# Gate and up projections: two blocks of 64 channels stacked on the 128 rows of TensorE, in place of gate on one half of the rows and up on the other

## The chip, the cores and the metric

The kernel runs on one core of a Trainium2 chip. Its instructions stand in five queues, each run in order: TensorE (PE in the profile, with its weight loads shown apart as PEld), VectorE (DVE), ScalarE (ACT), GpSimd (POOL) and SyncE (SP), which here issues all DMAs. The metric is the device time of one execution in microseconds (us), and the lower the better. It is given as the median of several runs. One further execution is profiled; all durations below come from it.

## The reference, cut to what matters

```python
x = x + ga * _A_ref(h, ...)      # spectral block over 8192 tokens of 448 channels, h = layernorm(x)*(1+ca)+sa
h = _layernorm(x, axis=-1) * (1 + cb) + sb
x = x + gb * ((_gelu(h @ w_gate) * (h @ w_up)) @ w_down)   # w_gate, w_up 448 x 1792; w_down 1792 x 448
```

The change concerns `h @ w_gate` and `h @ w_up` of the last line, what prepares their operands, and the traffic between memory and SBUF that goes with them. The spectral block, GELU and `w_down` are computed as before.

## The kernel before, in words

The first part (up to about 450 us in the profile) computes the spectral block in units of its own and, beside it, prepares the weights. The second part (450 us to the end) is the feed-forward loop.

**The loop.** The 8192 tokens make 32 chunks of two token groups of 128. The 1792 hidden features make seven tile pairs t of two times 128. A unit u is one chunk with one tile pair, so there are 224 units, and `period(u)` writes out the work around each. Odd chunks take the tile pairs in reverse (`torder`), so that some weights are still in SBUF.

**Seven products for eight.** For a unit, gate and up are each a product of 2 token groups x 448 channels with 448 channels x 2 tiles. The 448 channels are seven blocks of 64: two halves of three blocks (192 channels) and a rest of one. The halves are multiplied by Winograd's form of Strassen's scheme: seven products of halves in place of eight, with sums of weights (`form_sums`: S1 to S4) and of tokens (`token_sums`: t1 to t4). Each operand is split in f16 into a high and a low part, and each product adds three terms: high by high, weight high by token low, weight low by token high. `RV`, `RY`, `RX` are three regions of a PSUM set into which the products are added.

**Half rows.** Gate's weights lie in SBUF on partitions 0 to 63 and up's on 64 to 127. `mm` (L1171 to L1184, the product at L1177) issues, for each block of 64 channels and each of the three terms, one product on the upper 64 rows of the array (gate) and one on the lower 64 (up), each of 64 rows x 128 weights with 128 tokens. A unit has 25 blocks (`stage_a` 9, `stage_d` 4, `stage_c` 9, `stage_b` 3), so 25 x 3 x 2 = 150 products, each with a weight load of its own. As the block is needed on both halves of the rows, the tokens are transposed twice, shifted by 64 columns (`nt`, 2 x 24 blocks of 128 x 128, by DMA transposes at L1161).

**The order.** Within period u each engine takes: `stage_a(u)`, then on the unit two back `joins` (DVE, L1223 and L1229: PSUM plus a copy), `gel3` (ACT, L1235), `mult3` (DVE, L1239), `stage_d(u-2)`, `gel1` (ACT, L1243), `mult1` (DVE, L1246) and `sums` (POOL, L1250 to L1253), further `quant_hi(u-3)` (ACT, L1258) and `quant_lo(u-4)` (DVE, L1267), then `stage_c(u-1)` and `stage_b(u)`. `stage_d(u-2)` writes where `joins(u-2)` reads, so TensorE waits for it. `seed` and `copy_b` are ACT's copies L1218 and L1214. With k = u mod 7, the lists `extra` and `first` add the preparation of later chunks: `split_v`, `split_g` (k = 1), `transposes` of the next chunk (k = 1 to 4), `token_sums` (k = 3, 4) and packing into f16 (`pack_hi` on ACT, `pack_lo` on POOL, k = 3 to 6). After period k = 2, `phase` issues the `inverse` of the chunk after next (L1066 to L1068, 6 products) and `down` of the chunk before: 147 products with 224 columns each (L1277 to L1279), full rows.

**Weights.** The seven tile pairs do not all fit, so four slots hold them; after the last use in a chunk, `after` and `flush` put a reload on SP's queue (L1032, three parts). They come from a DRAM copy that the first part wrote (`store_forms`, L830). Tile pairs 0 and 1 are formed last and stay in the two slots in which they were formed.

Of the kernel before, what the change touches and what calls it, by code (L numbers as in the profile page):

```python
# [34 lines left out]
WPARTS = (12, 6, 5)  # L35
NWB = sum(WPARTS)
NXB = 48
NXT = NXB // 2
# [8 lines left out]
def spectral_geglu(ctx, tc, x, w1, b1, w2, b2, wg, wu, wd, cvec, wmod, cf1, cs2, cmi, cgm, out):  # L47
# [11 lines left out]
    wsd = [dram.tile([NP, 128, 2, n, 128], F16, name=f"wsd{n}") for n in WPARTS]  # L59
# [261 lines left out]
    with ExitStack() as bctx:  # L321
# [472 lines left out]
        def load_forms(t):  # L794
            r = fp.tile([128, 14, 128], F32, tag="wr", name="wr", bufs=2)
            for pr, rows in enumerate(rows2):
                v = (wg, wu)[pr].rearrange("(k p) (q t f) -> p q k t f", p=64, q=2, t=NP)
                for q in range(2):
                    dma(r[rows, 6 * q : 6 * q + 6], v[:, q, 0:6, t])
                dma(r[rows, 12:14], v[:, :, 6, t])  # L800
            return r

        def form_sums(t):
            r = raws[("w", t)]
            f = raws[("f", t)] = fp.tile([128, 9, 128], F32, tag="wf", name="wf")
            a11, a12, a21, a22 = (r[:, 3 * j : 3 * j + 3] for j in range(4))
            G.tensor_tensor(f[:, 3:6], a11, a21, ALU.subtract)
            G.tensor_tensor(a21, a21, a22, ALU.add)
            G.tensor_tensor(f[:, 0:3], a21, a11, ALU.subtract)
            G.tensor_tensor(f[:, 6:9], a12, f[:, 0:3], ALU.subtract)  # L810

        def form_cuts(t, part):
            r = raws[("w", t)]
            if part == 0:
                return (slice(0, 9), r[:, 0:9]), (slice(18, 23), r[:, 9:14])
            return ((slice(9, 18), raws[("f", t)]),)

        def forms_hi(t, part):
            for k, src in form_cuts(t, part):
                S.activation(wslot[wat[t]][:, 0, k], src, AF.Copy, scale=sww)  # L820

        def forms_lo(t, part):
            for k, src in form_cuts(t, part):
                w = wslot[wat[t]]
                V.scalar_tensor_tensor(w[:, 1, k], src, sww, w[:, 0, k], op0=ALU.mult, op1=ALU.subtract)

        def store_forms(t):
            a = 0
            for w, n in zip(wsd, WPARTS):
                dma(w[t], wslot[wat[t]][:, :, a : a + n])  # L830
                a += n
# [52 lines left out]
        wpool = ctx.enter_context(tc.tile_pool(name="wpool", bufs=1))  # L884
        wslot = [wpool.tile([128, 2, NWB, 128], F16, name=f"ws{s}") for s in range(2)]
# [85 lines left out]
        fp = fctx.enter_context(tc.tile_pool(name="fp", bufs=1))  # L971

# [28 lines left out]
    with ExitStack() as cctx:  # L1001
        cp = cctx.enter_context(tc.tile_pool(name="cp", bufs=1, side="right"))
        wslot += [cp.tile([128, 2, NWB, 128], F16, name=f"ws{s}") for s in (2, 3)]
# [5 lines left out]
        pkt = cp.tile([128, (NXB + 1) * 64], F16, name="pk")  # L1009
# [5 lines left out]
        def plan_slots():  # L1015

            held = [[0 if wat[0] == s else 1, -1] for s in range(2)] + [[2, -1], [3, -1]]
            for u, t in enumerate(torder):
                s = next((n for n, (h, _) in enumerate(held) if h == t), None)
                if s is None:  # L1020
                    s = min(range(4), key=lambda n: held[n][1])
                    refill[held[s][1]] = u
                    held[s][0] = t
                slot_of[u] = wslot[s]
                held[s][1] = u
# [3 lines left out]
        def load_part(u, part):  # L1029

            lo, n = sum(WPARTS[:part]), WPARTS[part]
            dma(slot_of[u][:, :, lo : lo + n], wsd[part][torder[u]])  # L1032
# [84 lines left out]
        def token_sums(i, part):  # L1117

            n = nxt[i]["n"]
            if part == 0:  # L1120
                nxt[i]["t"] = cp.tile([128, 13 * 64], F32, tag="tf", name="tf")
# [3 lines left out]
            t1, t2, t3, t4 = (t[:, 192 * j : 192 * j + 192] for j in range(4))  # L1125
            if part == 0:
                V.tensor_tensor(t1, b12, b11, ALU.subtract)  # L1127
                V.tensor_tensor(t3, b22, b12, ALU.subtract)
            else:
                V.tensor_tensor(t2, b22, t1, ALU.subtract)  # L1130
                V.tensor_tensor(t4, b21, t2, ALU.subtract)
                V.tensor_tensor(t[:, 768:832], x0, x1, ALU.subtract)

        def pieces(i, k):
            n, h = nxt[i]["n"], 448
            if k == 0:
                return n[:, 0], 0, 448, 448
            if k == 1:
                return n[:, 1, 192:448], 896, 256, 256
            t, a, b = nxt[i]["t"], *((0, 416), (416, 832))[k - 2]  # L1140
            return t[:, a:b], 1408 + a, 832, b - a

        def pack_hi(i, ks):
            for k in ks:
                src, o, _, w = pieces(i, k)
                S.copy(pkt[:, o : o + w], src)
                if k == 0:
                    S.copy(pkt[:, NXB * 64 :], src[:, 0:64])

        def pack_lo(i, ks, e=G):  # L1150
            for k in ks:
                src, o, d, w = pieces(i, k)
                e.tensor_tensor(pkt[:, o + d : o + d + w], src, pkt[:, o : o + w], ALU.subtract)

        def transposes(i, gs, w=4):
            if i not in nts:
                nts[i] = cp.tile([128, 2, NXT, 128], F16, tag="nt", name="nt", bufs=2)
            for g in gs:
                sw_, c = divmod(g, NXT // w)
                o, n = 64 * sw_ + 128 * w * c, 128 * w  # L1160
                nc.sync.dma_start(nts[i][:, sw_, w * c : w * c + w, :], pkt[:, o : o + n], transpose=True)  # L1161

        XB0, XB1, XT = (0, 7), (14 - 3, 18 - 3), (22, 35)

        def xblock(i, pr, n):
            w, odd = divmod(n, 2)
            if odd == pr:
                return nts[i][rows2[pr], 0, w, :]
            return nts[i][rows2[pr], 1, w if odd else (w - 1) % NXT, :]

        def mm(u, ps2, reg, wb, x, xo, n, start=False):  # L1171

            i, slot = u // NP, slot_of[u]
            for j in range(n):
                for m, (hl, xb) in enumerate(((0, x[0]), (0, x[1]), (1, x[0]))):
                    for pr, rows in enumerate(rows2):
                        T.matmul(  # L1177
                            ps2[:, pr, reg * 128 : reg * 128 + 128],
                            slot[rows, hl, wb + j, :],
                            xblock(i, pr, xb + xo + j),  # L1180
                            start=start and j == 0 and m == 0,
                            stop=j == n - 1 and m == 2,
                            skip_group_check=True,
                        )  # L1184

        RV, RY, RX = 0, 1, 2

        def stage_a(u):
            p = sets[u % 3]
            mm(u, p, RY, 0, XB0, 0, 3, start=True)  # L1190
            mm(u, p, RV, 6, XT, 0, 3)
            mm(u, p, RX, 3, XB0, 3, 3)

        def stage_b(u):
            mm(u, sets[u % 3], RY, 9, XT, 3, 3)

        def stage_c(u):
            p = sets[u % 3]
            mm(u, p, RV, 12, XT, 6, 3)
            mm(u, p, RV, 22, XB1, 6, 1)  # L1200
            mm(u, p, RY, 15, XB1, 3, 3)
            mm(u, p, RY, 21, XB1, 6, 1)
            mm(u, p, RX, 21, XB0, 6, 1)

        def stage_d(u):
            p = sets[u % 3]
            mm(u, p, RV, 18, XT, 9, 3)
            mm(u, p, RV, 22, XT, 12, 1)
# [127 lines left out]
        def period(u):  # L1336
# [8 lines left out]
            on(u - 2, lambda v: after(v, 2))  # L1345
# [5 lines left out]
            on(u - 1, lambda v: after(v, 1))  # L1351
# [7 lines left out]
        def phase(i):  # L1359
# [33 lines left out]
            2: [(token_sums, 1, 1), (pack_hi, 1, [2, 3]), (pack_lo, 1, [2, 3]), (transposes, 1, [0, 2], 12)],  # L1393
            3: [(transposes, 1, [1, 3], 12), ("inverse", 2), (residual, 2)],
# [3 lines left out]
            7: [(token_sums, 2, 1), (pack_hi, 2, [2, 3]), (pack_lo, 2, [2, 3])],  # L1398
        }
# [15 lines left out]
        cp2 = cctx.enter_context(tc.tile_pool(name="cp2", bufs=1))  # L1415
        loads(1)
        for part in range(len(WPARTS)):
            load_part(2, part)
        for b in range(CB):
            norm2(0, b)  # L1420
            if b == 0:
                pack_hi(0, [0])
                pack_lo(0, [0])
        token_sums(0, 0)
        token_sums(0, 1)
        pack_hi(0, [2, 3])
        pack_hi(0, [1])
        pack_lo(0, [2, 3], V)
        pack_lo(0, [1])
        S.copy(gb_r, gb[:, :D])  # L1430
        transposes(0, range(4), 12)
        for part in range(len(WPARTS)):
            load_part(3, part)
# [103 lines left out]
```

## Time and profile before

| | before |
|---|---|
| median of 3 runs | 2095.89 us (2095.4 to 2103.03) |
| the profiled execution, its own time | 2103.25 us |
| its span, first to last instruction | 2101.4 us |
| first product of the loop (L1177) | 449.65 us |
| mean granted TensorE clock | 0.969 of full speed |
| VectorE, ScalarE, GpSimd busy | 70%, 49%, 53% of the span |
| DMA: packets, bytes, share of the 16 engines | 390171, 358.5 MB, about 73% |

Times in rows of the trace are in us from the start of the span. A row of the timeline has start, length, engine, line, operation, output<-inputs, shape, count, and in brackets the idle time of the engine before it and what ended it. "issue" means that the engine waited for nothing that the profile shows. A matmul's record runs some 200 ns longer than the time until the next one can start, as they are pipelined. So the pace of a row with n matmuls is its length, less one record, by n - 1.

### The profile page before, as it was taken

What the parts mean: (1) busy time and instruction counts of PE and PEld (TensorE: products, weight loads), DVE (VectorE), ACT (ScalarE), POOL (GpSimd) and SP (SyncE); (2) the same over time, 40 slices, a digit from 0 to 9 for tenths busy, and PEclk for the clock granted to TensorE, in tenths of its full rate; (3) what the DMA queues carried; (4) which work ended last, traced back from release to release, by engine and by line L of the source; (5) the groups of instructions that cost most, each with busy time, mean ns of one, the idle gap of its engine ahead of it and who ended that gap; (6) DMA issues with size and microseconds to landing.
All of it is one profiled execution on the core that took longest, in us unless ns stands there. A gap on an engine that the chain in (4) does not pass through costs nothing.

```text
span 2101.4 us, 93045 instructions
## 1 busy us (share of the span) xinstructions
PE 1871.1 (89%) x41348; PEld 1781.5 (85%) x41348; DVE 1479.4 (70%) x2958; ACT 1029.4 (49%) x1917; POOL 1116.5 (53%) x1529
## 2 busy tenths in 40 slices
PE   7899878768989999899899998999989999999998
PEld 3699877757989888888898998898889889888998
DVE  8577777757767767666677776777667667677645
ACT  5587776634444444444444444444444444444433
POOL 3166666425555556555555655555555556555533
PEclk9899988979999999999999999999999999999999
DMA  9998688687766667767666677877666667777671
GB/s 344 305 283 244 163 237 235 184 233 177 148 148 148 148 148 148 148 148 148 148 148 148 161 158 149 154 158 156 148 148 148 148 148 164 150 166 147 142 157 40
DMA packets 390171, 358.48 MB, mean 171 GB/s; under 512 B 223876, under 2 KB 341256, under 8 KB 389768
## 3 DMA queue, kind: packets, MB, share of 16 engines
q1 hardware_dynamic: 389768, 352.53, 71.3%
q8 instruction: 323, 5.29, 1.1%
q14 instruction: 80, 0.66, 0.2%
HBM read 244.24 MB, written 57.80 MB: 144 GB/s over the span
## 4 chain that ended last, share of the span: by engine, by line
PE 69%; DVE 17%; issue 6%; DMA 3%; ACT 2%; SPq 2%; POOL 0%; ACTq 0%; DVEq 0%; POOLq 0%
PE set L1177 35%; PE pdn L1277 4%; PE pdn L1279 4%; PE pdn L1278 4%; PE set L1279 3%; PE set L1277 3%; PE set L1278 3%; DVE x L1239 3%; DVE c L1223 2%; DVE ac L1267 2%; PE ps L204 2%; DVE y L465 1%; DVE c L1229 1%; DVE tf L1127 1%; DMA g<-cgm 1%
## 5 line engine op out<-in xcount | busy, mean ns | idle before, releaser
L1177 PE MATMUL set<-nt,ws 64*128 64x128 f16 x33600 | 996.5, 218 | 147.9 <-issue 100.7
L1177 PEld LDWEIGHTS <-ws 64*128 64x128 f16 x33600 | 968.0, 95 | 176.9 <-issue 167.0
L1267 DVE SCALAR_TENSOR_TENSOR ac<-x,sa_act,ac 128x896 f16<-128x896 f32 x224 | 318.6, 1422 | 16.0 <-ACT ac L1258 15.9
L1235 ACT ACTIVATE gl<-c,dg 128x384 f32<-128x384 f32 x224 | 137.7, 615 | 370.8 <-DVE c L1229 358.3
L1223 DVE TENSOR_TENSOR c<-set,sb 128x512 f32<-128x512 f32 x224 | 153.6, 686 | 120.4 <-PE set L1177 111.6
L1277 PE MATMUL pdn<-wd,ac 128*128 128x224 f16 x896 | 233.6, 261 | 1.1 <-issue 0.6
L1279 PE MATMUL pdn<-wd,ac 128*128 128x224 f16 x896 | 233.1, 260 | 1.2 <-DVE ac L1267 1.2
L1278 PE MATMUL pdn<-wd,ac 128*128 128x224 f16 x896 | 233.1, 260 | 0.0
L1258 ACT ACTIVATE ac<-x,sa_act 128x896 f16<-128x896 f32 x224 | 231.4, 1033 | 0.5 <-DVE x L1253 0.4
L1250 POOL TENSOR_TENSOR x<-x 128x128 f32<-128x128 f32 x223 | 106.0, 475 | 221.6 <-DVE x L1239 221.6
L1239 DVE TENSOR_TENSOR x<-c,gl 128x384 f32<-128x384 f32 x224 | 198.9, 888 | 28.2 <-ACT gl L1235 28.0
L1321 POOL TENSOR_TENSOR o<-u,p 128x224 f32<-128x224 f32 x32 | 21.1, 659 | 325.9 <-DVE u L1320 325.9
L1214 ACT COPY sb<-set 128x512 f32<-128x512 f32 x224 | 129.8, 580 | 102.7 <-PE set L1177 102.4
L1277 PE MATMUL set<-wd,ac 128*128 128x224 f16 x672 | 174.0, 259 | 0.1
L1279 PE MATMUL set<-wd,ac 128*128 128x224 f16 x672 | 174.0, 259 | 0.0
L1278 PE MATMUL set<-wd,ac 128*128 128x224 f16 x672 | 174.0, 259 | 0.0
L1277 PEld LDWEIGHTS <-ac 128*128 128x128 f16 x1568 | 153.9, 98 | 8.2 <-issue 6.7
L1279 PEld LDWEIGHTS <-ac 128*128 128x128 f16 x1568 | 153.8, 98 | 2.0 <-DVE ac L1267 1.7
L1278 PEld LDWEIGHTS <-ac 128*128 128x128 f16 x1568 | 154.0, 98 | 1.3 <-issue 1.0
L465 DVE SCALAR_TENSOR_TENSOR y<-pm,t 64x224 f32<-64x224 f32 x256 | 99.5, 389 | 59.6 <-ACT t L457 55.9
L1246 DVE TENSOR_TENSOR x<-set,gl 128x128 f32<-128x128 f32 x224 | 63.9, 285 | 94.5 <-ACT gl L1243 94.1
L109 POOL TENSOR_TENSOR yl<-y,yh 128x448 fp32r<-128x448 f32 x63 | 81.1, 1287 | 92.3 <-ACT yh L107 74.1
(293 smaller groups left out, 3684.8 us busy)
## 6 DMA issues: line engine op xcount, KB each, us to landing
ws<-wsd SPq DMA_DIRECT2D x98, 768.0 KB, 5.5
ws<-wsd SPq DMA_DIRECT2D x98, 384.0 KB, 5.6
ws<-wsd SPq DMA_DIRECT2D x98, 320.0 KB
tr<-td SPq DMA_DIRECT2D x64, 224.0 KB, 5.5
vd<-us SPq DMA_DIRECT2D x64, 224.0 KB, 3.0
xx<-in_A_x SPq DMA_DIRECT2D x32, 448.0 KB, 6.0
v<-vd SPq DMA_DIRECT2D x63, 224.0 KB, 3.6
out<-x SPq DMA_DIRECT2D x31, 448.0 KB, 2.7
```

The lines of the kernel that those rows point to most:

```text
L465: V.scalar_tensor_tensor(y[ri * 64 : ri * 64 + 64, gi], pv[si, ri], LAM, tv[si, ri], op0=ALU.add, op1=ALU.min)
L1177: T.matmul(ps2[:, pr, reg * 128 : reg * 128 + 128], slot[rows, hl, wb + j, :], xblock(i, pr, xb + xo + j), start=start and j == 0 and m == ...
L1214: S.copy(sbs[u], sets[u % 3][:, :, 0:256])
L1223: V.tensor_tensor(c[:, :, 1:3, :], p[:, :, 0:256].rearrange("p g (r c) -> p g r c", r=2), b[:, :, 0:128].rearrange("p g (o c) -> p g o c", ...
L1235: S.activation(gls[u], cts[u][:, 0], AF.Gelu_apprx_tanh, scale=dg)
L1239: V.tensor_tensor(xs[u][:, 1::3, :], cts.pop(u)[:, 1], gls.pop(u), ALU.mult)
L1250: e.tensor_tensor(s1, a21, a22, ALU.add)
L1258: S.activation(acts[u][:, 0], xs[u][:, 0:7], AF.Copy, scale=sa_act[:, t : t + 1])
L1267: V.scalar_tensor_tensor(acts[u][:, 1], xs.pop(u)[:, 0:7], sa_act[:, t : t + 1], acts[u][:, 0], op0=ALU.mult, op1=ALU.subtract)
L1277: T.matmul(ps, ac[:, 0, ka], w[:, 0, kb], start=n == 0, stop=False)
L1278: T.matmul(ps, ac[:, 0, ka], w[:, 1, kb], start=False, stop=False)
L1279: T.matmul(ps, ac[:, 1, ka], w[:, 0, kb], start=False, stop=n == NP - 1)
```

## The change

Each product now uses all 128 rows: two blocks of 64 channels of the same projection stand one above the other. Gate and up become two products in turn (`pr`) with weights of their own. A product of halves has three blocks and three terms, 9 half tiles, and takes 5 full-row products (A11, S1, S2); with the rest block it has 12 half tiles and takes 6 (A12, S4, S3, A22). That is (3 x 5 + 4 x 6) x 2 = 78 products per unit, of 128 rows x 128 weights with 128 tokens. In the 5-product form the third block's token tile holds its high part above its low part.

What goes with it:

- The tokens need one layout of 25 blocks, transposed once, by 5 DMA transposes of 5 blocks per chunk and no longer 12 of 4. All are issued at k = 1 and 2. `pieces` packs five pieces, some with two strided parts; GpSimd makes 7 subtractions per chunk where there were 4, and one copy of 64 columns more.
- A tile pair's weights in SBUF are 2 x 2 x 14 tiles (projection, high or low part, form), 14336 bytes per partition, where there were 11776. They are reloaded in two parts of 1024 descriptors each (1024 and 768 bytes), where there were three of 256 (3072, 1536, 1280 bytes).
- `store_forms` writes a tile pair by 16 DMAs and no longer 3, `load_forms` reads the raw weights by 10 and no longer 6. The forms are made in two staging buffers of their own, so tile pairs 0 and 1 are loaded from DRAM at the start of the loop as well.

```diff
-WPARTS = (12, 6, 5)
-NWB = sum(WPARTS)
-NXB = 48
-NXT = NXB // 2
+NWB = 23
+WPARTS = ((0, 4), (4, 7))
+NXT = 25
...
         def store_forms(t):
-            a = 0
-            for w, n in zip(wsd, WPARTS):
-                dma(w[t], wslot[wat[t]][:, :, a : a + n])
-                a += n
+            w = wstage[wat[t]]
+            for pr, rows in enumerate(rows2):
+                top, low = (wk[t, r, pr] for r in rows2)
+                dma(top[:, :, 0:7], w[rows, :, 0:7])
+                dma(top[:, :, 7:14], w[rows, :, 14:21])
+                dma(low[:, :, 0:7], w[rows, :, 7:14])
+                dma(low[:, :, 8:11], w[rows, :, 15:18])
+                for f, b in ((7, 21), (11, 21), (12, 22), (13, 22)):
+                    dma(low[:, :, f], w[rows, :, b])
...
-            lo, n = sum(WPARTS[:part]), WPARTS[part]
-            dma(slot_of[u][:, :, lo : lo + n], wsd[part][torder[u]])
+            view = lambda w: w.rearrange("p r l (g f) x -> p (r l g) f x", g=2)[:, :, slice(*WPARTS[part])]
+            dma(view(wslot[slot_of[u]]), view(wk[torder[u]]))
...
-        def mm(u, ps2, reg, wb, x, xo, n, start=False):
-
-            i, slot = u // NP, slot_of[u]
-            for j in range(n):
-                for m, (hl, xb) in enumerate(((0, x[0]), (0, x[1]), (1, x[0]))):
-                    for pr, rows in enumerate(rows2):
-                        T.matmul(
-                            ps2[:, pr, reg * 128 : reg * 128 + 128],
-                            slot[rows, hl, wb + j, :],
-                            xblock(i, pr, xb + xo + j),
...
+        def mm(u, reg, f, x, start=False):
+
+            ps2, slot, nt = sets[u % 3], wslot[slot_of[u]], nts[u // NP]
+            if f in (A11, S1, S2):
+                terms = [(0, f, x), (0, f, x + 2), (1, f, x), (0, 7 + f, x + 1), (1, 7 + f, x + 1)]
+            else:
+                terms = [(l, f + 7 * g, x + g + 2 * m) for g in range(2) for l, m in ((0, 0), (0, 1), (1, 0))]
+            for j, (hl, wt, xt) in enumerate(terms):
+                for pr in range(2):
+                    T.matmul(
+                        ps2[:, pr, reg * 128 : reg * 128 + 128],
+                        slot[:, pr, hl, wt, :],
+                        nt[:, xt, :],
...
         def stage_a(u):
-            p = sets[u % 3]
-            mm(u, p, RY, 0, XB0, 0, 3, start=True)
-            mm(u, p, RV, 6, XT, 0, 3)
-            mm(u, p, RX, 3, XB0, 3, 3)
+            mm(u, RY, A11, B11, start=True)
+            mm(u, RV, S1, T1)
+            mm(u, RX, A12, B21)
...
-            1: [(2, split_v), (2, split_g), (1, transposes, [0, 6])],
-            2: [(1, transposes, [1, 7, 11, 5, 2, 8])],
-            3: [(1, transposes, [3, 9]), (2, token_sums, 0), (2, pack_hi, [0]), (2, pack_lo, [0])],
-            4: [(1, transposes, [4, 10]), (2, token_sums, 1), (2, pack_hi, [1]), (2, pack_lo, [1])],
-            5: [(2, pack_hi, [2]), (2, pack_lo, [2])],
-            6: [(2, pack_hi, [3]), (2, pack_lo, [3]), (3, load_v)],
+            1: [(2, split_v), (2, split_g), (1, transposes, [0])],
+            2: [(1, transposes, range(1, 5))],
+            3: [(2, token_sums, 0), (2, pack_hi, [0, 1]), (2, pack_lo, [0, 1])],
+            4: [(2, token_sums, 1), (2, pack_hi, [2]), (2, pack_lo, [2])],
+            5: [(2, pack_hi, [3]), (2, pack_lo, [3])],
+            6: [(2, pack_hi, [4]), (2, pack_lo, [4]), (3, load_v)],
```

With the other stages likewise: `stage_b` is S2, `stage_c` S3 and S4, `stage_d` A22. So in products the stages have 32 (a), 12 (d), 24 (c) and 10 (b), where they had 54, 24, 54 and 18.

**SP's queue at the start of the loop.** Before, from the store of the tile pair formed last (wsd_60 to wsd_62 are its three parts in DRAM) to the first transposes:

```order
L830 DMA wsd_60<-ws_3352 256x1x1536
L830 DMA wsd_61<-ws_3352 256x1x768
L830 DMA wsd_62<-ws_3352 256x1x640
L934 DMA v<-vd 128x2x224 x2
L926 DMA g<-cgm 128x256
L928 DMA xx<-in_A_x 128x896
L1032 DMA ws_5801<-wsd_60 128x2x1536
L1032 DMA ws_5801<-wsd_61 128x2x768
L1032 DMA ws_5801<-wsd_62 128x2x640
L1161 DMA_TRANSPOSE nt<-pk 128x12x128 x4
```

Now (the second half of the tile pair's store, then as far; the first half has the same five rows; wk_5916 and wk_5917 are the slots of units 0 and 1):

```order
L836 DMA wk<-ws_3365 64x2x896
L837 DMA wk<-ws_3365 64x2x896
L838 DMA wk<-ws_3365 64x2x896
L839 DMA wk<-ws_3365 64x2x384
L841 DMA wk<-ws_3365 64x2x128 x4
L942 DMA v<-vd 128x2x224 x2
L934 DMA g<-cgm 128x256
L936 DMA xx<-in_A_x 128x896
L1041 DMA wk_5916<-wk 128x8x512
L1041 DMA wk_5916<-wk 128x8x384
L1041 DMA wk_5917<-wk 128x8x512
L1041 DMA wk_5917<-wk 128x8x384
```

The five transposes follow it. So thirteen more stores and one more load stand ahead of the first transposes, and the weights of units 0 and 1 are loaded where they lay in SBUF.

**SP's queue in one chunk of the loop.** Before, around the output of one chunk (`out<-x`, issued at the end of `down`):

```order
L1032 DMA ws_5801<-wsd_60 128x2x1536
L1161 DMA_TRANSPOSE nt<-pk 128x4x128 x6
L1328 DMA out<-x_5897 128x896
L1032 DMA ws_3352<-wsd_62 128x2x640
L1032 DMA ws_5801<-wsd_61 128x2x768
L1161 DMA_TRANSPOSE nt<-pk 128x4x128 x2
L1032 DMA ws_5801<-wsd_62 128x2x640
L1161 DMA_TRANSPOSE nt<-pk 128x4x128 x2
```

Now, at the same place:

```order
L1175 DMA_TRANSPOSE nt<-pk 128x5x128
L1041 DMA wk_5984<-wk 128x8x384
L1041 DMA wk_5916<-wk 128x8x512
L1175 DMA_TRANSPOSE nt<-pk 128x5x128 x4
L1334 DMA out<-x_8019 128x896
L1041 DMA wk_5917<-wk 128x8x384
L1041 DMA wk_5916<-wk 128x8x384
```

The transposes that stood behind the output of the chunk before (k = 3 and 4) now stand ahead of it, and each tile pair has two reloads and no longer three.

More of the change, by code (lines that the diff above doesn't have):

```diff
@@ L58, in spectral_geglu @@
     sd = dram.tile([NP, 128, 4, HC], F32, name="sd")
[L59 removed]
+    wk = dram.tile([NP, 128, 2, 2, 14, 128], F16, name="wk")
     cpool = ctx.enter_context(tc.tile_pool(name="cpool", bufs=1))
@@ L971, in spectral_geglu @@
         fp = fctx.enter_context(tc.tile_pool(name="fp", bufs=1))
+        wstage = [fp.tile([128, 2, NWB, 128], F16, name=f"ws{s}") for s in range(2)]
         at(18, "dve", down_scales)
```

149 lines of the change are left out of this document (75 added, 74 removed).

## The prediction

> **What bounds the kernel now.** I read the page first: how busy TensorE is, whose work makes up the chain that ended last, and how many instructions there are.
>
> ```profile
> span 2101.4 us, 93045 instructions
> PE 1871.1 (89%) x41348; PEld 1781.5 (85%) x41348; DVE 1479.4 (70%) x2958; ACT 1029.4 (49%) x1917; POOL 1116.5 (53%) x1529
> q8 instruction: 323, 5.29, 1.1%
> PE 69%; DVE 17%; issue 6%; DMA 3%; ACT 2%; SPq 2%; POOL 0%; ACTq 0%; DVEq 0%; POOLq 0%
> L1177 PE MATMUL set<-nt,ws 64*128 64x128 f16 x33600 | 996.5, 218 | 147.9 <-issue 100.7
> ```
>
> TensorE carries the chain, over a third of it with the products that are changed. But 6% of the chain is "issue", and the products' largest idle time has that name. The second view is TensorE's timeline over one chunk, with the first product after a `down` early and late in the loop:
>
> ```profile
> 530.51 0.68 PE L1177 MATMUL set<-nt,ws 64*128 64x128 f16 x18 [0.48 <-DVE o L1325]
> ...
> 1151.75 10.06 PE L1177 MATMUL set<-nt,ws 64*128 64x128 f16 x354 [0.48 <-DVE o L1325]
> 1162.55 4.82 PE L1177 MATMUL set<-nt,ws 64*128 64x128 f16 x158 [0.73 <-DVE c L1229]
> 1167.92 11.07 PE L1177 MATMUL set<-nt,ws 64*128 64x128 f16 x384 [0.54 <-issue]
> 1179.15 3.97 PE L1177 MATMUL set<-nt,ws 64*128 64x128 f16 x128 [0.17 <-issue]
> 1184.27 0.90 PE L1177 MATMUL set<-nt,ws 64*128 64x128 f16 x26 [1.15 <-issue]
> 1185.10 0.47 PE L1066 MATMUL set<-vh,gh 128*128 128x448 f32 x1
> ...
> 2010.40 0.79 PE L1177 MATMUL set<-nt,ws 64*128 64x128 f16 x22 [0.48 <-DVE o L1325]
> ```
>
> From 530.51 to 2010.40 lie 29 chunks (periods 10 to 213), 51.03 us each. I cut a chunk in three: **A**, from the first product to `stage_d` in the period k = 5 (here 1151.75 to 1162.55, 10.80 us); **B**, the rest of the products; **C**, inverse, `down` and the wait for DVE, until the next first product (1201.18). The windows view gives the engines in A, B, C of that chunk:
>
> ```profile
> 1151.75:1162.55 10.80, 10.06 (x354) 9.92 (x354) 10.08 (x17) 6.41 (x14) 9.97 (x14) 1.00 0.68 124
> 1162.55:1185.10 22.55, 20.59 (x697) 19.64 (x696) 16.59 (x24) 15.40 (x28) 13.99 (x22) 1.00 0.64 174
> 1185.10:1201.18 16.08, 15.60 (x156) 15.15 (x154) 9.19 (x30) 0.97 (x3) 4.82 (x7) 1.00 0.78 155
> ```
>
> Columns: window, length, then busy time (and count) of PE, PEld, DVE, ACT, POOL; last the clock and DMA. **A** is VectorE's: 10.08 of 10.80 busy (`token_sums`), and TensorE waits at its end (0.73 us for DVE c). **B** is TensorE's, as DVE needs 16.6, ACT 15.4, POOL 14.0 of 22.55 us. **C** is `down`.
>
> What is "issue"? Two rows of another chunk:
>
> ```profile
> 1026.62 3.75 PE L1177 MATMUL set<-nt,ws 64*128 64x128 f16 x128 [1.65 <-issue]
> 1033.67 0.21 PE L1177 MATMUL set<-nt,ws 64*128 64x128 f16 x1 [3.29 <-issue]
> ...
> q8 instruction: 272, 4.46, 1.3%
> ```
>
> Between two such waits stand 128 products, and 384 = 3 x 128 in the chunk above. The DMA queue q8 brings instructions (its rows give packets, MB and share): 5.29 MB over the 2 x 41348 of TensorE is 64 bytes each, and 5.29 MB over 323 packets is 16 KB, or 256 instructions: 128 products with their weight loads. So TensorE runs a block empty, and the next is not there. From 530.51 to 2010.40 (last row) that is 272 blocks, 9.4 per chunk. Products run at (3.75 - 0.21)/127 = 27.9 ns, so a block lasts 3.57 us, and 3.57 + 3.29 = 6.9 us is the slowest refill of these rows.
>
> The Trainium skill ("Runtime: NRT & Kernel Launch", Instruction fetch mechanics) has the same 16 KiB blocks of 256 instructions, but calls their cost mostly hidden. By that rule these waits would be something else, and the change would not touch them; the trace's runs of 128 speak against it. It is the slower rival below.
>
> **The change part by part.**
>
> *Pace of a product.* A pair of half-row products runs at the same time: 2 x 27.9 = 55.8 ns. What does one full-row product with 128 columns cost? The first part has some, 24 in a row from L370 to L372, and full 128 x 128 loads at L716:
>
> ```profile
> 269.62 0.22 PE L370 MATMUL ps<-s,th 128*112 128x128 f16 x1
> ...
> 270.90 0.22 PE L372 MATMUL ps<-s,tl 128*112 128x128 f16 x1
> ...
> 200.77 0.48 PE L716 MATMUL pw<-onesb,sq 128*128 128x1 bf16 x7
> ...
> L716 PE MATMUL pw<-onesb,sq x112: 163/164/179, 118.1 to 219.3; 128*128 128x1 bf16 x84, 64*128 64x1 bf16 x28
> ...
> L1277 PEld LDWEIGHTS <-ac 128*128 128x128 f16 x1568 | 153.9, 98 | 8.2 <-issue 6.7
> ```
>
> 23 steps in 1.28 us: 55.7 ns, each with its own full-row load. The L716 products have one column and a record of 163 ns (second L716 row, minimum); seven in 0.48 us come every (0.48 - 0.16)/6 = 53 ns, so a 128-wide load needs no more than that. So 55.7 ns, hence 78 x 55.7 = 4.34 us per unit for 75 x 55.8 = 4.18: **the products by themselves get 4% longer**. Bounds: 55.7, and 98 ns (the record of a 128 x 128 load in `down`, last row) if loads were not hidden.
>
> *Part A.* TensorE needs 2 x 78 + 32 = 188 products, 10.47 us, under 10.80; DVE's instructions there are the same, so A stays 10.80. POOL's packing there changes a little: three subtractions of 64, 128 and 256 columns where one of 448 stood, and a copy of 64 columns more.
>
> ```profile
> L1250 POOL TENSOR_TENSOR x<-x 128x128 f32<-128x128 f32 x223 | 106.0, 475 | 221.6 <-DVE x L1239 221.6
> ```
>
> At 0.48 us for 128 columns that is some 0.5 us more on 9.97 of 10.80 busy. DVE's order does not wait for it, but POOL beside DVE may lengthen DVE's instructions: 0 to 0.5, I take 0.
>
> *Part B.* 46 products are left of the period k = 5, then 4 x 78: 358 x 55.7 = 19.95 us. Before, 348 pairs made 19.4. The remaining ~3.1 us of 22.55 in this chunk were waits; in the mean chunk B is 51.03 - 10.80 - 16.08 = 24.15 (fetches in A and C counted in it), so 4.7 are.
>
> *Do the waits go?* A block now holds 128 full-row products, 128 x 55.7 = 7.13 us, and the slowest refill above took 6.9. Per chunk 699 products make 5.5 blocks. I expect nearly all to go and leave 0.2 us per chunk. Bounds: none go (4.7 left), or all.
>
> *Part C.* Same instructions, 16.08; TensorE's change of tile shape (64 rows to 128) falls away: the last half product starts 0.21 before the end of its row, at 1184.96, and the inverse 0.14 later, where a step is 0.06. That is 0.1 us.
>
> Chunk after: 10.80 + 20.15 + 16.0 = 46.95, **4.08 less, times 29 = 118 us**. The last chunk (from 2010.40) runs into the end of the program, and I take half of a chunk's gain for it: 2 us.
>
> *What then stands late.* In B, DVE has 16.6 us of work for 20.0, ACT 15.4, POOL 14.0 plus some packing: all fit, DVE the tightest.
>
> *DMA.* Transposes fall from 48 to 25 blocks per chunk, weights rise by 14336/11776 = 1.22 in bytes and in packets of 1 KB for 3 KB. Both lie behind three or more periods (13 us) between slot free and next use:
>
> ```profile
> ws<-wsd SPq DMA_DIRECT2D x98, 768.0 KB, 5.5
> nt<-pk SPq DMA_TRANSPOSE x368, 5.1
> ```
>
> Landing after 5.5 us leaves over 7 us. If reloads took three times as long, `stage_a` would wait; 0 to 3 us per chunk, and I take 0.
>
> *The start.* These rows set when the loop begins:
>
> ```profile
> 432.18 3.60 SPq L830 DMA_DIRECT2D wsd<-ws  x3
> 435.88 1.81 SPq L934 DMA_DIRECT2D v<-vd  x2
> 438.79 2.03 SPq L1032 DMA_DIRECT2D ws<-wsd  x3
> 442.55 9.67 SPq L1161 DMA_TRANSPOSE nt<-pk  x4
> 454.59 1.68 PE L1177 MATMUL set<-nt,ws 64*128 64x128 f16 x28 [4.68 <-DMA nt<-pk]
> ```
>
> Sixteen stores at about 0.6 us (a `v` load takes 0.9, a part load 0.7) are 9.6 for 3.6; four loads for three, 0.7 more. The transposes start 6 to 7 us later, but 5 of 5 blocks are shorter than 4 of 12, and the first stage needs three of them: 2 to 5 us late, I take 3. In the first part each tile pair puts 17 more DMAs on SP, some 10 us at 0.6 each, and SP has idle time there:
>
> ```profile
> SPq L516 <- ACT us L499: 68.6, 13, 8.8
> ```
>
> (waits of SP from 200 to 450 us): 0 to 15 us in all, I take 3. The added fixed costs of strided forms on ACT and DVE are under 1 us. The first ten periods, 449.65 to 530.51, also lose fetch waits, but are DVE's in large part; I take 0.
>
> **Sum.** 2103.25 - 118 - 2 + 6 = 1989, rounded **1990 us**. The profiled execution is 7 us above the median of the runs; one of the three is as long, so I leave it.
>
> **The rivals.**
>
> *Waits stay (slower).* If "issue" is bound to traffic and not to the count of instructions, only the longer products remain: B + 0.56 us, times 30 = 17, and 6 at the start: **2126**. It decides where fewer than about 0.75 us of waits per chunk go (0.56 and the start's 0.2). For it: the long waits lie beside transposes and reloads. Against: runs of 128 and multiples, which no traffic makes. 0.05.
>
> *Loads not hidden (slower).* At 98 ns per product A takes 18.4 and B 35.1 us, a chunk 69.6, +18.6 x 30: **2660**. Against it stand the 55.7 ns of L370 to L372. 0.02. The Trainium skill ("TensorE: Matmul & The Clock Gate", Back-to-back issue gap) has 81 ns for such a stream of load and product; by that, an estimate, A 15.2, B 29.0, and about 2390 us. The trace disagrees, at 55.7.
>
> *Another bound in B.* When TensorE no longer pauses, DVE beside POOL sets B: at A's rate, 10.8 us for 2.4 periods, 4.5 per period, B's 4.6 periods take 20.7 to 22; or a late reload costs 1 to 2 us. Half the gain is lost: **2035 to 2050**. For it: DVE at 83% of the new B. Against: the row with x384 ran 11.07 us, 4.32 us per 150 products and so per period, nearly the new 4.34, with no wait for DVE. 0.13.
>
> **How the numbers follow.** Forecast 0.78 (1966 to 2025); another bound 0.13 (2025 to 2080); waits stay 0.05; loads 0.02; unknown 0.02 on either side of no change. The range reaches from 1966 (all waits gone, no cost at the start, against the median of runs) to 2045, which leaves out 2 in 10 with the tails. Faster by over 0.5% 0.91, slower by over 0.5% 0.07, between 0.02; 0.5% is about what a measurement of this kernel can tell from no change.
>
> **What would show it.** Right: products' "issue" waits under 10 us in all (100.7 now), q8 near 200 packets, full-row products 55.7 ns apart, A 10.8 and B 20.2, first product near 453 to 458. Wrong: waits for DVE c or DMA wk inside B, steps of 80 to 100 ns, "issue" as now, or a first part longer by over 10 us.

## The result, and the profile after

| | before | after |
|---|---|---|
| median of 3 runs | 2095.89 us | 2042.14 us (2037.63 to 2044.26) |
| ratio, with its 95% interval | | 0.9729 (0.9688 to 0.977) |
| the profiled execution, its own time | 2103.25 us | 2044.26 us |
| first product of the loop | 449.65 us | 512.72 us |
| from there to the end of the span | 1651.8 us | 1529.3 us |
| a chunk, mean of 29 | 51.03 us | 47.13 us |

The change is 2.7% faster; the forecast was 1990 us, 5% faster. The table splits the difference of the profiled executions, 59 us: the loop won 122.5 us (forecast 120), and the first part lost 63.1 (forecast 6). So nearly all of the miss lies ahead of the loop. That the loop's sum came so near is partly luck: the 29 chunks gave 113.2 us (forecast 118), the first ten periods 5.4 (forecast 0) and the end 3.9 (forecast 2).

The loop first. Page of the changed kernel, the lines that answer to those of before:

```profile
span 2042.0 us, 60539 instructions
PE 1861.7 (91%) x25220; PEld 1793.1 (88%) x25220; DVE 1495.1 (73%) x2966; ACT 1036.7 (51%) x1924; POOL 1228.5 (60%) x1656
q8 instruction: 197, 3.23, 0.7%
PE 72%; DVE 9%; DMA 8%; SPq 6%; ACT 2%; issue 2%; POOL 0%; ACTq 0%; DVEq 0%; POOLq 0%
L1192 PE MATMUL set<-nt,wk 128*128 128x128 f16 x17472 | 990.9, 219 | 47.7 <-DVE o L1331 14.9
```

Half as many products have nearly the busy time of before (990.9 us for 996.5). What fell is their idle time, 147.9 to 47.7 us, and "issue" is no longer its first releaser. q8 moved 197 blocks of instructions for 323. In the chain "issue" fell from 6% to 2%, while SPq rose from 2% to 6% and DMA from 3% to 8%. One chunk, cut into A, B and C as in the prediction, by the windows view (same columns):

```profile
588.19:598.68 10.49, 10.49 (x188) 10.49 (x188) 9.46 (x17) 6.86 (x14) 10.18 (x17) 1.00 0.53 162
598.68:619.17 20.49, 20.32 (x361) 20.02 (x358) 17.05 (x24) 15.29 (x28) 16.34 (x24) 1.00 0.49 160
619.17:635.26 16.09, 15.61 (x154) 15.15 (x155) 10.42 (x31) 0.97 (x3) 6.02 (x8) 1.00 1.04 183
```

A and B are now TensorE's: 10.49 of 10.49 and 20.32 of 20.49 us busy. 188 products in 10.49 us are 55.8 ns each, the pace that the prediction took from L370 to L372.

Now the first part. The waits view from 245 to 455 us, the stretch in which weights are formed beside the spectral units (us in all, times, longest):

```profile
DVE y L464 <- ACT t L456: 77.7, 17, 13.1
PE pm L442 <- ACT hh L432: 55.2, 7, 11.1
ACT wd L970 <- DMA dr<-in_B_w_down: 44.7, 6, 10.2
ACT wd L970 <- DMA dr<-sd: 12.4, 6, 2.7
```

and the kernel before, from 245 to 410 us:

```profile
DVE y L465 <- ACT t L457: 33.5, 18, 5.2
PE pm L443 <- ACT hh L433: 6.4, 6, 3.8
ACT wd L962 <- DMA dr<-in_B_w_down: 5.8, 2, 4.5
ACT wd L962 <- DMA dr<-sd: 1.6, 3, 1.1
```

`down_hi` (L970), which scales the weights of `down` into f16, waits for its raw data `dr` for 57 us in place of 7. ScalarE runs in order, so `hh` and `t` of the spectral unit stand behind it, and TensorE and VectorE wait for those. Why is `dr` late? SP's queue in one tile pair's two steps, timeline of the changed kernel:

```profile
290.48 1.29 SPq L335 DMA_DIRECT2D tr<-td  x2
291.87 0.55 SPq L343 DMA_DIRECT2D s<-cs  x1
292.52 0.59 SPq L836 DMA_DIRECT2D wk<-ws  x1
...
302.00 3.02 SPq L841 DMA_DIRECT2D wk<-ws  x4
305.06 1.94 SPq L798 DMA_DIRECT2D wr<-in_B_w_gate  x3
...
312.32 0.61 SPq L800 DMA_DIRECT2D wr<-in_B_w_up  x1
313.02 0.54 SPq L916 DMA_DIRECT2D dr<-in_B_w_down  x1
313.60 0.47 SPq L917 DMA_DIRECT2D dr<-in_B_w_down  x1
314.17 0.38 SPq L918 DMA_DIRECT2D dr<-sd  x1
...
325.14 1.30 SPq L335 DMA_DIRECT2D tr<-td  x2
```

with ScalarE's answer on its own timeline:

```profile
316.78 0.85 ACT L970 ACTIVATE wd<-dr,dsc 128x672 f16<-128x672 f32 x1 [9.18 <-DMA dr<-in_B_w_down]
```

From 292.52 SP issues 16 stores (to 305.02) and 10 reads (to 312.93) without a pause, and only then the three loads of `dr` of the same step. From `tr` (290.48, the token transforms' input of the next step) to the same place two steps on (325.14) lie 34.7 us, where the kernel before took 24.6:

```profile
297.09 1.89 SPq L336 DMA_DIRECT2D tr<-td  x2
...
310.70 2.58 SPq L830 DMA_DIRECT2D wsd<-ws  x3
...
318.84 0.54 SPq L908 DMA_DIRECT2D dr<-in_B_w_down  x1
...
321.68 1.88 SPq L336 DMA_DIRECT2D tr<-td  x2
```

There `dr` stood 8.1 us behind the first store (310.70 to 318.84), now 20.5 us. In the two steps SP issued 22 DMAs in 15.0 us, now 39 in 27.0 us.

The 63.1 us add up. Against the kernel before, the changed one is 4.0 us ahead at the step before the first store of forms (`tr` at 245.2 for 249.2), then loses 50.8 us over five tile pairs (`tr` at 418.8 for 372.0), 10.2 each, and 2.1 more to the store of the tile pair formed last (481.10 for 432.18). From that store to the first product it takes 31.6 us for 17.5, 14.1 more. -4.0 + 50.8 + 2.1 + 14.1 = 63.0. The last piece on SP:

```profile
481.10 0.61 SPq L836 DMA_DIRECT2D wk<-ws  x1
...
493.86 1.05 SPq L942 DMA_DIRECT2D v<-vd  x2
...
496.00 8.44 SPq L1041 DMA_DIRECT2D wk<-wk  x4
504.55 9.87 SPq L1175 DMA_TRANSPOSE nt<-pk  x5
```

12.8 us of stores stand for 3.6, and the four loads of weights take 8.44 us on the queue where the three of before took 2.03.

### The profile page after: what moved, and what is told of

The parts are those of the page before. It is cut to its first block, busy times and chain, and to the rows that moved or that the text cites. A ratio compares the mean times of both kernels' runs of the same rounds, so it can differ in the third digit from the quotient of the medians.

```text
span 2042.0 us, 60539 instructions
## 1 busy us (share of the span) xinstructions
PE 1861.7 (91%) x25220; PEld 1793.1 (88%) x25220; DVE 1495.1 (73%) x2966; ACT 1036.7 (51%) x1924; POOL 1228.5 (60%) x1656
## 4 chain that ended last, share of the span: by engine, by line
PE 72%; DVE 9%; DMA 8%; SPq 6%; ACT 2%; issue 2%; POOL 0%; ACTq 0%; DVEq 0%; POOLq 0%
PE set L1192 39%; DMA g<-cgm 5%; PE pdn L1283 4%; PE pdn L1285 4%; PE pdn L1284 4%; PE set L1285 3%; PE set L1283 3%; PE set L1284 3%; PE ps L203 2%; SPq L841 2%; DVE y L464 2%; DVE ac L1273 1%; DMA dr<-sd 1%; SPq L798 1%; DVE c L1229 1%
## 5 line engine op out<-in xcount | busy, mean ns | idle before, releaser
L1192 PEld LDWEIGHTS <-wk 128*128 128x128 f16 x17472 | 983.6, 98 | 59.1 <-issue 51.5
L1192 PE MATMUL set<-nt,wk 128*128 128x128 f16 x17472 | 990.9, 219 | 47.7 <-DVE o L1331 14.9
L1273 DVE SCALAR_TENSOR_TENSOR ac<-x,sa_act,ac 128x896 f16<-128x896 f32 x224 | 326.1, 1456 | 10.8 <-ACT ac L1264 10.2
L1245 DVE TENSOR_TENSOR x<-c,gl 128x384 f32<-128x384 f32 x224 | 212.8, 950 | 29.3 <-ACT gl L1241 29.3
L1256 POOL TENSOR_TENSOR x<-x 128x128 f32<-128x128 f32 x223 | 108.1, 485 | 127.0 <-DVE x L1245 127.0
L1259 POOL TENSOR_TENSOR x<-x 128x128 f32<-128x128 f32 x223 | 132.5, 594 | 2.5 <-DVE x L1252 2.5
```

The lines of the kernel that those rows point to most:

```text
L1192: T.matmul(ps2[:, pr, reg * 128 : reg * 128 + 128], slot[:, pr, hl, wt, :], nt[:, xt, :], start=start and j == 0, stop=j == len(terms) - 1 ...
L1245: V.tensor_tensor(xs[u][:, 1::3, :], cts.pop(u)[:, 1], gls.pop(u), ALU.mult)
L1259: e.tensor_tensor(s4, a12, s2, ALU.subtract)
L1273: V.scalar_tensor_tensor(acts[u][:, 1], xs.pop(u)[:, 0:7], sa_act[:, t : t + 1], acts[u][:, 0], op0=ALU.mult, op1=ALU.subtract)
```

## The experiments

The kernel before, run beside these, took 2080.9 us (one execution, beside dr first, stores spread, fewer stores and density), then 2084.63 us (median of 7, beside the run of both edits, the order 0 to 6 and the changed kernel again) and 2083.93 us (median of 11, beside the timed run of both edits and the run with unit 1 later). Each group ran on a chip of its own. A total without "median" is one execution; seven executions of the changed kernel lie between 2037.63 and 2046.27 us. The changed kernel beside the second group:

> The changed kernel unedited, on the same chip and beside the same runs of the kernel before, so that the experiments can be compared with it on one chip: ratio 0.97, first product at 508 to 515 us.

It took 2043.05 us (median of 4), ratio 0.9781 (0.9716 to 0.9845), first product at 514.66 us.

**dr first.** Only the place of three loads in the program is changed:

```diff
+        for t, u in enumerate([21, 23, 25, 27, 29, 30, 31]):
+            at(u - 1, "load" if u < 30 else "pool", load_d4, t)
         for n, t in enumerate(worder):
...
         for t, u in enumerate([21, 23, 25, 27, 29, 30, 31]):
-            at(u - 1, "load" if u < 30 else "pool", load_d4, t)
             at(u, "act", down_hi, t)
```

> Only the order on SP is changed: the three loads of dr stand ahead of the 16 stores and 10 reads of their step and no longer behind them. In the changed kernel the first product of the loop starts at 512.7 us, and two steps of the first part take 34.6 us, in which SP issues for 27.0 us (28.5 with the gaps between two DMAs). Theory 1 (order: ScalarE's in-order down_hi waits for dr, which stands behind the stores): the waits of L970 for dr go (57 us now), the pitch falls to between 24.5 us, the pace before the change, and SP's 28.5, so over some 5.5 tile pairs 33 to 55 us are won: first product at 458 to 480, total 1989 to 2012 us. Rival (count: SP has too many DMAs in whatever order): the pitch stays above 32 us, other loads (tr, wr) are late in place of dr, first product above 500, total above 2028. Rival (landing: the transfers themselves are slow, not their place in the queue): the waits for dr stay at over 5 us each, total above 2028.

2011.35 us, first product at 480.15, the pitch of two steps 28.5 us. Waits view from 245 to 455 us:

```profile
ACT th L106 <- DMA tr<-td: 29.8, 5, 7.0
ACT wd L970 <- DMA dr<-in_B_w_down: 5.8, 2, 5.3
```

The order theory holds, and so does its limit. The waits for `dr` go from 57 to 7.5 us (the 5.8 above and 1.7 for `dr<-sd`), and the first product comes 32.6 us earlier. On the same chip the density run below, whose first part is the changed kernel's, has it at 510.94, which makes 30.8. But the next load in the queue, `tr`, is late in its place. SP is full: 39 DMAs in 26.1 us of issue, with some 65 ns between two of them, make the 28.6 us from one `tr` (314.56) to the next (343.13). Where the transfers themselves were slow, moving three loads would have won nothing; that rival falls. The count rival is wrong of the changed kernel (28.5 is not 34.6) and right of this one.

**Stores spread over two steps.**

```diff
-                at(u + 2, "load", store_forms, t)
+                at(u + 2, "load", store_forms, t, (0,))
+                at(u + 3, "load", store_forms, t, (1,))
```

> The 16 stores of a tile pair are split over two steps: gate's eight in the step where all stood, up's eight in the next, which has no reads. dr stays behind what is left. Theory 1 (order): about 6.2 us of stores no longer stand ahead of dr, so its wait falls from 10 to 4 us per tile pair: first product 475 to 490, total 2005 to 2020. Rival (count): the number of DMAs per two steps is the same, so pitch and total stay: 2038 to 2048. Rival (landing): the same, 2038 to 2048.

2017.97 us, first product at 486.69. The same 39 DMAs with the same bytes, in another order: the first product comes 26 us earlier, or 24.3 against the 510.94 of the same chip. The waits for `dr` fall to 31.0 us (17.1 and 13.9, some 5 per tile pair; 4 were expected). Count and landing would both have given no change.

**Fewer stores.** `form_cuts` writes the 28 blocks of the copy in DRAM into the staging buffer, in their order, so that four stores carry a tile pair (two small tiles, `gh` and `gl`, change pools to make room):

```diff
-                dma(top[:, :, 0:7], w[rows, :, 0:7])
-                dma(top[:, :, 7:14], w[rows, :, 14:21])
-                dma(low[:, :, 0:7], w[rows, :, 7:14])
-                dma(low[:, :, 8:11], w[rows, :, 15:18])
-                for f, b in ((7, 21), (11, 21), (12, 22), (13, 22)):
-                    dma(low[:, :, f], w[rows, :, b])
+                v = w[rows].rearrange("p l (g r f) x -> p r (l g) (f x)", g=2, r=2)
+                for n, r in enumerate(rows2):
+                    dma(wk[t, r, pr].rearrange("p l (g f) x -> p (l g) (f x)", g=2), v[:, n])
```

> The staging buffer holds 28 blocks in the order of the copy in DRAM (the five blocks that stand there twice are written twice by ScalarE and VectorE), so a tile pair is stored by 4 DMAs of 128 packets... and not by 16; ScalarE and VectorE get three short instructions more per tile pair each, some 1.5 us. dr stays behind the stores. Theory 1 and the count rival agree that it helps: SP's issue per two steps falls by 12 x 0.7 = 8.5 us, dr waits 1 to 2 us and no longer 10, pitch near 26: first product 450 to 470 (the last tile pair's store ahead of the transposes is 9 us shorter as well), total 1980 to 2002 us. Rival (landing): the same bytes are stored and read, so if the bytes in flight make dr late, the start stays above 500 and the total above 2028; but the 256 byte packets are gone as well, so a part of it could go.

2007.96 us, first product at 479.82, a pitch of 28.9 us: faster, but less than the 450 to 470 expected. Two rows of SP's timeline say why:

```profile
316.35 5.37 SPq L845 DMA_DIRECT2D wk<-ws  x4
321.76 4.60 SPq L798 DMA_DIRECT2D wr<-in_B_w_gate  x3
```

A store of the four costs SP 1.34 us in the mean, not 0.7, and the three reads behind them 4.6 us for 1.94. Each of the four has 256 pieces of 1792 bytes, not the 128 expected; but taken one by one, the first two took 0.59 us each and the other two 2.00, so their size alone does not set the time. What makes SP wait there was not tried. So the stores and three reads ended 10.0 us after the first store (316.35 to 326.36), where the changed kernel needed 14.5 (292.52 to 307.00): 4.5 us saved and not 8.5. `dr` still stands behind them and is waited for 25.4 us in all (14.9 and 10.5).

**Both.**

> Both edits together: 4 stores per tile pair and the three loads of dr ahead of them. In the run with dr first alone the pitch of two steps was 28.4 us and SP never paused in it; 16 stores took 13.3 us of that, and 4 wide ones take 5.4 us. Theory 1 (SP's time is the bound once the order is right): SP's share falls to about 20.5 us per two steps, so SP no longer binds and the pitch is the 24.5 us of before the change, or 25 to 26 with the added short instructions of ScalarE and VectorE; first product at 452 to 465 us, total 1975 to 1992 us on a chip where the one edit alone gave 2011 and the other 2008. Rival (the bound behind SP is ScalarE or VectorE, which form more products of the same weights): the pitch stays at 28 to 29 us and the first product at 475 to 480, total 2003 to 2010.

1987.67 us, first product at 458.45. `tr` stands at 278.4, 303.5, 329.2, 352.8 and 376.5 us: 24.5 us for two steps, the pace of before the change. ScalarE and VectorE were not behind SP as a bound. The first product is 56.2 us earlier than in the changed kernel on the same chip (514.66), and 9 us behind the 449.65 of before (on another chip). The same version again:

> The version with wide stores and dr first once more, timed: it gave 1987.7 us in one execution beside 2084.6 of the kernel before. Theory: 55 us under the changed kernel (2043 on that chip), ratio to the kernel before 0.953, between 0.948 and 0.958; first product at 455 to 462 us, two steps of the first part 24.5 us.

1989.90 us (median of 6, 1987.4 to 1995.2), ratio to the kernel before 0.956 (0.953 to 0.959), first product at 460.63. This beats both kernels: 53 us under the 2043.05 of the changed one.

**The loop's start.** Two tries to bring the first transposes forward, on top of that version. In the first, the tile pairs are formed in the order 0 to 6, and the last store is moved behind the transposes:

```diff
-        worder = list(range(2, NP)) + [0, 1]
+        worder = list(range(NP))
...
-        store_forms(worder[-1])
-        fctx.close()
-        cp2 = cctx.enter_context(tc.tile_pool(name="cp2", bufs=1))
...
         transposes(0, range(5))
+        store_forms(worder[-1])
+        fctx.close()
+        cp2 = cctx.enter_context(tc.tile_pool(name="cp2", bufs=1))
...
```

> As the run with both edits, and the tile pairs are formed in the order 0 to 6 and no longer 2 to 6, 0, 1, so that units 0 and 1 can be loaded ahead of the last store; that store stands behind the first transposes. Ahead of the transposes SP then has four loads and v, g, xx (12 us) and no stores (5.6 us in the run with wide stores). Theory (the first transposes wait for SP, as pk is ready some 8 us before they are issued): the first product comes 5 to 6 us earlier than in the run with both edits, total 1969 to 1987 us. Rival (the transposes wait for pk or for the weights' landing anyway): no gain, or the weights of units 2 and 3, loaded behind the store, stop TensorE for 3 to 5 us in the first periods: the same total as the run with both edits or up to 5 us more.

1994.21 us (median of 4), ratio 0.9543 (0.9489 to 0.9598). The first product came at 456.13, 2.3 us earlier than in the untimed run of the version it builds on. Then the timeline of TensorE shows the rival:

```profile
458.76 4.40 PE L1197 MATMUL set<-nt,wk 128*128 128x128 f16 x76 [0.67 <-ACT sb L1225]
473.85 10.13 PE L1197 MATMUL set<-nt,wk 128*128 128x128 f16 x156 [10.69 <-DMA wk<-wk]
```

The weights of unit 2 go into the memory of the staging buffer, which is free only when the store has left it; TensorE waits 10.7 us for them, for 3 to 5 expected, and nothing is won. In the second try only the two loads of unit 1 go behind the transposes:

> As that version, but the two loads of unit 1's weights stand behind the first transposes and no longer ahead of them. Ahead of the transposes SP had 6.65 us of weight loads. Theory (pk is ready earlier, SP is what the transposes wait for): they start 3 us earlier, first product 3 us earlier, and unit 1's weights arrive as the first unit ends, total 0 to 3 us less, which is under what the runs can tell. Rival (unit 1's weights come late): a wait for wk of 3 to 8 us in the first two periods, total 0 to 6 us more.

1990.68 us (median of 6), ratio 0.9554 (0.9528 to 0.958): no difference from the version it builds on. The first product came at 455.34, 5.3 us earlier than there, but the first product of period 10 at 533.64 for 532.90: the gain is gone within ten periods. Counted from start to start of products, the steps that wait for VectorE's `c` make 6.2 us for 3.5 and those that wait for weights 5.4 for 4.1; the rest was not traced. VectorE's work for chunk 1 (`rct`) starts at 455 us in both, so an earlier first product does not bring it forward.

**Density of instructions.** To show what the loop's gain was, gate and up are issued as four products over half the rows, two each (each leaves out half of its stacked channels and adds the other half twice):

```diff
-                for pr in range(2):
+                for n, pr in enumerate((0, 1, 0, 1)):
...
-                        slot[:, pr, hl, wt, :],
-                        nt[:, xt, :],
+                        slot[rows2[pr], pr, hl, wt, :],
+                        nt[rows2[pr], xt, :],
```

> Each pair of full-row products (gate, up) is issued as four products over half the rows, gate on the upper 64 and up on the lower 64, each twice; so gate sums only the upper half of the stacked channels, doubled, and up only the lower half, doubled. TensorE's pace in time, the DMAs, the weights in SBUF and all else stay as in the changed kernel; only the instructions per microsecond double, to the density before the change (156 products per unit, 27.9 ns each). Theory (instruction blocks: a 16 KB block lasts 3.57 us and the next is not there yet): the issue waits return, some 130 us over the program, and q8 rises to above 320 packets; chunk about 51 us, total 2150 to 2180. Rival (traffic: the waits before came from transposes and reloads that the change thinned out): no issue waits, chunk 47.1, total 2036 to 2050.

2226.83 us, chunk 53.11 us, first product at 510.94 as in the changed kernel. Page and TensorE's timeline:

```profile
q8 instruction: 334, 5.47, 1.0%
L1192 PE MATMUL set<-nt,wk 64*128 64x128 f16 x34944 | 1041.7, 220 | 162.8 <-issue 125.4
...
1078.33 9.89 PE L1192 MATMUL set<-nt,wk 64*128 64x128 f16 x348 [0.48 <-DVE o L1331]
1089.59 3.75 PE L1192 MATMUL set<-nt,wk 64*128 64x128 f16 x128 [1.37 <-issue]
1093.61 14.47 PE L1192 MATMUL set<-nt,wk 64*128 64x128 f16 x512 [0.28 <-issue]
1111.08 4.41 PE L1192 MATMUL set<-nt,wk 64*128 64x128 f16 x104 [3.00 <-issue]
```

With the changed kernel's transfers, slots and transposes, doubling the instructions alone brings the waits back, at 128 and 512 = 4 x 128 products. That settles the cause: blocks of 128 products, not traffic. The Trainium skill ("Runtime: NRT & Kernel Launch", Instruction fetch mechanics) calls the cost of fetching these blocks mostly hidden; here it is hidden at 55.7 ns per product and not at 27.9, so the measurement decides against that rule for a stream as dense as this one. The size was missed: 2150 to 2180 had been expected. The page's 125.4 us is what was expected; beside it, counted from the starts of the products in the 29 chunks, 635 steps took 0.1 to 0.2 us where a pair takes 0.06, nearly all of them in series, every second step. 625 of the 635 lie in stretches of 3.4 us in which the granted clock is half of full speed. The windows view of one of them, the clock being the third number from the end:

```profile
530.23:533.65 3.42, 3.42 (x72) 3.42 (x68) 0.06 (x1) 1.05 (x3) 0.48 (x2) 0.50 1.12 351
```

The same view over the 29 chunks, for the kernel before, the changed kernel and this run:

```profile
530.51:2010.40 1479.89, 1352.93 (x34881) 1313.02 (x34881) 1042.18 (x1979) 664.97 (x1274) 824.30 (x1186) 0.99 0.72 152
588.19:1954.90 1366.71, 1341.09 (x20266) 1322.68 (x20266) 1059.58 (x1979) 669.41 (x1274) 935.59 (x1302) 1.00 0.67 168
590.87:2130.99 1540.12, 1396.35 (x36100) 1357.49 (x36100) 1049.37 (x1979) 673.10 (x1274) 875.45 (x1302) 0.97 0.61 150
```

The kernel before has 12 such stretches in them (41 us), this run 23 (78 us), the changed kernel none. Counted from the products' starts, half clock made the products of the kernel before 17 us longer, and those of this run 29. So some 17 of the 113.2 us that the chunks won came from the clock and not from the waits themselves. As this run differs from the changed kernel in the products alone, twice as many over half the rows, they bring back both. Whether it is the waits or the half rows that lower the clock is not shown.

## Why the prediction was right or wrong

*Products at 55.7 ns.* Right: 188 in 10.49 us. The 81 ns of the Trainium skill ("TensorE: Matmul & The Clock Gate", Back-to-back issue gap) would have made these 15.2 us, an estimate; the trace has 10.49.

*The waits go because a block lasts 7.13 us.* Right, and shown by the density run. What is left of "issue" is 81 steps of 8.6 us in all from start to start, 4.1 us more than at the products' pace, and the forecast was under 10. But the 4.7 us per chunk that were taken for waits held some 0.6 us of products at half clock (17 us in 29 chunks), which the prediction did not see. They went as well, so part of the right number is luck.

*Part A stays 10.80 as VectorE's.* Wrong by 0.31 us, to the good: it is TensorE's, 10.49. VectorE's 17 instructions took 10.08 us in the chunk shown before and take 9.46 in this one. So the busy share of an engine that works beside others was taken for a limit and was none; why its instructions became shorter was not tried.

*Parts B and C.* B 20.61 us in the mean for a forecast of 20.15, C 16.03 for 16.0. In B TensorE now waits for ScalarE's copy `seed` (L1224), as the groups of instructions show, with more releasers in the row than the page has:

```profile
L1192 PE MATMUL set<-nt,wk 128*128 128x128 f16 x17472 | 990.9, 219 | 47.7 <-DVE o L1331 14.9 <-ACT set L1224 12.0 <-DMA nt<-pk 10.1
```

Measured from start to start of the products it is 17.1 us over their pace in 29 waits, some 0.6 per chunk; before the change it was 3.7 us in all. A, B and C together give the 47.13 us of a chunk for 46.95. The rival "another bound in B" did not come: VectorE's `c` was late for 4.1 us in all, and after the first units no product waits for a reload. In the view of DMA issues the second part of a reload lands as soon as the reloads of before (5.5 us); for the first part the trace has only two landings, both at the loop's start, so their median says nothing of the loop:

```profile
wk<-wk SPq DMA_DIRECT2D x100, 1024.0 KB, 12.1
wk<-wk SPq DMA_DIRECT2D x100, 768.0 KB, 5.4
```

The total, 2042 us, lies in the 2035 to 2050 of that rival all the same: a total alone would have spoken for it, and only the split between loop and first part speaks against it. Its price was also high by its own figures: B at 20.7 to 22 us for 20.15, times 30, is 17 to 56 us over the forecast, so 2006 to 2045.

*The start.* Here the prediction failed. Its paragraph put 17 more DMAs of a tile pair at "some 10 us at 0.6 each" on SP, set against it SP's idle time, "68.6, 13, 8.8", and took 3 us of 0 to 15 for the first part and 3 us for the transposes: the +6 of the sum. Measured are +49 and +14. Three steps in it were wrong. First, the idle time was read as a total and not held against the load: 68.6 us of waits stood against seven times 10 us, and per two steps 15.0 us of issue plus 10.2 and the gaps are already over the 24.6 us that two steps took. The added issue was 12.0 us. Second, only the length of the queue was counted and not what stands behind the new DMAs: `dr`, which ScalarE waits for in order. The dr-first run shows that this order alone cost 31 to 33 us, and the combined version that order and count together cost 56.2 (514.66 to 458.45), ahead of the loop and at its start. Third, the loads of 1024 descriptors were taken at 0.7 us each, from the 0.7 of a part load of before; four of them took 8.44 us, and the sixteen stores ahead of them 12.8 for 9.6.

So the sum, 1989 us, was 55 us under the profiled execution: the start gave 57 (63 for 6), and the loop took 2.5 of them back (122.5 for 120). That 2042 us still lies in the stated range is luck: its upper part was there for a late reload or a busy VectorE in B, and neither came. Its lower end was to be all waits gone and no cost at the start, against the median; added up, that gives 1970 and not 1966. That the version without this loss runs at 1989.9 us is in part chance, as the chips of that batch ran the kernel before 0.6% faster.

## What to carry to other kernels

When a change adds DMAs to a queue, sum the queue's issue time over one period of the loop around it and compare it with the period; an idle total over the whole stretch hides that it is full. Then list what is issued behind the new DMAs in the same step, and which engine waits for that in order: a load that is needed soon goes ahead of stores that nobody waits for. And where products come in runs of a fixed count with "issue" between them, fewer and larger instructions pay more than their own time.

## What had not been expected of the hardware

A DMA's time on SP is not one number, and its size does not give it. A store of 128 pieces took 0.59 us behind a quiet stretch. The four wide stores of 256 pieces took 0.59, 0.59, 2.00 and 2.00 us. The weight loads take 0.53 us in the median; the four at the loop's start took 0.58, 0.73, 4.05 and 2.94 us, 8.44 in all. The stores ahead of them are not the whole reason, as four such loads took 5.62 us in the run with the order 0 to 6, where no store of weights stands ahead of them (0.59, 0.66, 1.40 and 2.83). In these three bursts the first two are quick and the other two wait; what for was not tried. The wait also passes on to whatever stands behind: three reads took 4.6 us for 1.94.

The granted clock depends on how the same work is issued: in the 29 chunks the half-row products at 27.9 ns met stretches of half clock (41 us in the kernel before, 78 us in the density run), the full-row products at 55.7 ns none. What sets them off was not tried.
